# Attention and two experts on one core: two PSUM banks declared independent, all steps in a new order

## The chip, the cores and the metric
The kernel runs on 1 core of a Trainium2 chip. Five engines work side by side, each in the order of its own instruction stream: TensorE (PE, matmuls into PSUM; its weight loads are the rows PEld), VectorE (DVE), ScalarE (ACT), GpSimd (POOL) and SyncE (SP), which issues the DMAs. An instruction starts when the one before it on its engine has been started or is done and the semaphores that it waits for have been raised by other engines. [...]

The metric is the time of one execution on the device in microseconds. A profiled execution of the same kernel gives the trace; its span runs from the first to the last recorded instruction and is a little shorter than the execution's time.

## What is computed
Three stages follow each other. The first is causal attention with a bias from running sums of `s`, for 4 batches, 8 heads, 576 positions and 64 dimensions. The second and third are two experts over the resulting 2304 tokens of 512 values.

```python
# attention, for each batch and head
scores = scale * q @ k.T                     # 576 x 576
cum = cumsum(maximum(s, 0))
scores = where(causal, -1e9, scores + minimum(-(cum[:, None] - cum[None, :]), 0))
attn = exp(scores - max(scores)); attn /= sum(attn) + 1e-9
x = attn @ v                                 # gathered to 2304 x 512
# first expert
h = x @ w_in                                 # 512 -> 2048
x = (h - tanh(h)) @ w_out                    # 2048 -> 512
# second expert
h = x @ w2_in                                # 512 -> 1024
e = exp(h - max(h)); solu = h * e / (sum(e) + 1e-9)
ln = (solu - mean(solu)) / sqrt(var(solu) + 1e-6) * g_ln
out = ln @ w2_out                            # 1024 -> 512
```

All values are float32.

## The kernel before
**Split values.** [...] Each operand is kept as two parts: a rounded one ("hi", written by a CAST, on ScalarE in the rows below) and what is left ("lo", a subtraction, on VectorE in the rows below). A product is then three matmuls: hi times hi, hi times lo, lo times hi. Weights are brought into the same form by some steps on ScalarE and VectorE after their load: a magnitude (line 421), two to four integer steps (lines 403 to 414), a rounding (line 293) and a subtraction (line 317). For the weights w2_out of the second expert a scaling by the gain (line 499) stands in between.

**Attention** takes the heads in pairs. For a pair, TensorE makes the scores (line 719), turns the exponentials by transposes (line 785) and multiplies them with v (line 825); VectorE adds the bias (line 736), ScalarE takes the exponential (line 747) and copies the turned blocks (`pt`), GpSimd divides by the sum (line 751). `bc` is the running sum, spread over the partitions by a DMA from `cum_d`. Ahead of it stand "fillers", matmuls on a tile `junk` whose result nobody reads (line 562).

**First expert** (`expert1`). It works on blocks of 256 tokens, nine of them. Weights for 16 parts f of the hidden width are held in three visits: f 0 to 3 and f 4 to 7 (`VISITS`), whose partial sums go by way of `pd` in DRAM, and f 8 to 15 (the set `wb`). Each f of a block has an h step (line 872, 12 matmuls of 256 columns), a tanh (877), a subtraction (881), a rounding and a rest (293, 317: the tile `gh`), and an x2 step (line 895, 12 matmuls). The weights for `wb` replace buffers of attention, so that their first load (`cd<-in_moe_w_in_dram` at that place) waits for the end of attention. In the last visit line 957 adds the earlier partial sum to the result.

**Second expert** (`products`, `expert2`). For each of the nine blocks of 256 tokens the product with w2_in is made from seven products of half size, p1 to p7, in place of eight, in sums and differences of halves. A product is six matmuls of 512 columns (line 1013). Four of them go to a pair of banks, `big` (`Z["h"]`): p1 and p2 to bank 0, p5 and p3 to bank 1. p6, p7 and p4 go to a bank `b`. Between them the steps are, by their names in the code: k1 copies bank 0 behind p1, u2 = b + k1 (line 1029), k5 copies bank 1 behind p5, k15 adds the two copies (a line 317 with `hc<-hc`), u4 adds u2 into bank 1 (line 1044); then p2 adds into bank 0 and p3 into bank 1. TensorE's order within a block is p1, p6, p5, p2, p3, p7, p4. The two halves of 128 tokens are then two tiles, o = 0 and 1, with the exponential (line 1075), the product with h (1083), mean and variance (1088, 1092), the centring (1095), the reciprocal root (1100 to 1102, then three Newton iterations of three instructions, lines 1107 to 1109, on values of 128x1), eight transposes (1115), the split of what they give (`cd`, `cu`: 293 and 1122, called hi and lo of the first and the second half) and 24 matmuls with w2_out (1129).

**What sets the order.** The kernel first makes a list of 3302 steps, each with one or more ways to be done (on which engine). `ORDER`, a stored text, says in which order the steps are emitted and which way each takes: every word is a number to base 36, three times the step plus the way, and "+n" stands for n fillers. All engines' streams follow from this one order. The costs in the code (`t_pe`, `t_act`, ...) were used when `ORDER` was made; `Plan.order` doesn't use them. Which instruction waits for which follows from the tiles that the instructions read and write, in the order of emission: an instruction that writes a tile waits for the earlier ones of other engines that read or wrote it. The pair of banks is one tile. So u4, which reads and writes bank 1, waits for a p2 that stands ahead of it in the order, which writes bank 0. Whether p2 stands ahead is the order's choice.

## Time and profile before
| what | us |
|---|---|
| median of 3 executions | 791.61 (791.07, 791.61, 792.75) |
| the profiled execution | 792.16 |
| its span in the trace | 790.38 |
| TensorE busy in the span | 771.3 |
| VectorE busy | 541.4 |
| ScalarE busy | 412.6 |
| GpSimd busy | 156.0 |

The profiled execution took 1.8 us more than its span, and lies 0.55 us above the median of the three. An engine's busy time is the time in which at least one of its counted instructions ran; matmuls overlap at their ends, so that TensorE's busy time is not the sum of its matmuls. The granted clock of TensorE was 0.999 of full speed in the mean.

### The profile page before, as it was taken

What the parts mean: (1) busy time and instruction counts of PE and PEld (TensorE: products, weight loads), DVE (VectorE), ACT (ScalarE), POOL (GpSimd) and SP (SyncE); (2) the same over time, 40 slices, a digit from 0 to 9 for tenths busy, and PEclk for the clock granted to TensorE, in tenths of its full rate; (3) what the DMA queues carried; (4) which work ended last, traced back from release to release, by engine and by line L of the source; (5) the groups of instructions that cost most, each with busy time, mean ns of one, the idle gap of its engine ahead of it and who ended that gap; (6) DMA issues with size and microseconds to landing.
All of it is one profiled execution on the core that took longest, in us unless ns stands there. A gap on an engine that the chain in (4) does not pass through costs nothing.

```text
span 790.4 us, 16621 instructions
## 1 busy us (share of the span) xinstructions
PE 771.3 (98%) x6235; PEld 681.0 (86%) x6235; DVE 541.4 (68%) x1521; ACT 412.6 (52%) x1028; POOL 156.0 (20%) x321
## 2 busy tenths in 40 slices
PE   8899999999999999999999999999999999999998
PEld 5565788888898899999999898888899899989876
DVE  6887988854554366985699998765465664564773
ACT  6779988766666445554355664333142333333332
POOL 4334433322331100000000001122041202021112
PEclk9999999999999999999999999999999999999999
DMA  6999979867445379875445431012012101201001
GB/s 189 300 284 252 329 219 290 271 184 215 123 121 165 105 226 292 278 244 181 160 131 183 136 111 48 15 54 92 16 43 65 41 15 66 95 1 41 15 27 41
DMA packets 90033, 111.90 MB, mean 142 GB/s; under 512 B 11792, under 2 KB 74256, under 8 KB 89952
## 3 DMA queue, kind: packets, MB, share of 16 engines
q1 hardware_dynamic: 89952, 110.83, 45.7%
q8 instruction: 49, 0.80, 0.4%
q14 instruction: 32, 0.26, 0.1%
HBM read 87.11 MB, written 23.70 MB: 140 GB/s over the span
## 4 chain that ended last, share of the span: by engine, by line
PE 80%; DVE 10%; ACT 4%; DMA 2%; issue 2%; SPq 1%; POOL 0%; ACTq 0%; DVEq 0%; POOLq 0%
PE t L872 20%; PE t L1129 12%; PE acc L895 11%; PE big L895 10%; PE big L1013 6%; PE t L825 5%; PE t L785 4%; PE b L1013 4%; PE t L719 4%; PE t L1115 2%; ACT U L747 1%; DVE ct L414 1%; DVE U L736 1%; DVE ct L409 1%; ACT pt L293 1%
## 5 line engine op out<-in xcount | busy, mean ns | idle before, releaser
L872 PE MATMUL t<-xb,wih 128*128 128x256 f32 x1152 | 203.4, 279 | 0.1
L872 PEld LDWEIGHTS t<-xb,wih 128*128 128x128 f32 x1152 | 175.6, 188 | 2.2 <-DVE m L736 0.3
L872 PE MATMUL t<-xb,wil 128*128 128x256 f32 x576 | 160.0, 278 | 0.0
L751 POOL TENSOR_SCALAR U<-U,r 128x256 f32<-128x256 f32 (+8 forms) x144 | 85.8, 608 | 174.5 <-DVE r L663 72.9
L872 PEld LDWEIGHTS t<-xb,wil 128*128 128x128 f32 x576 | 108.7, 189 | 0.0
L895 PE MATMUL acc<-gh,woh 128*128 128x256 f32 x576 | 104.7, 283 | 1.2 <-DVE gh L317 1.1
L895 PE MATMUL big<-gh,woh 128*128 128x256 f32 x576 | 101.2, 278 | 0.6 <-DVE xp L957 0.6
L881 DVE TENSOR_TENSOR g<-t,th 128x256 f32<-128x256 f32 x144 | 59.8, 418 | 52.4 <-ACT th L877 51.2
L293 ACT CAST gh<-g 128x256 fp32r<-128x256 f32 x144 | 58.0, 406 | 67.9 <-DVE g L881 30.1
L877 ACT ACTIVATE th<-t 128x256 f32<-128x256 f32 x144 | 55.0, 383 | 71.1 <-PE t L872 66.5
L895 PEld LDWEIGHTS acc<-gh,woh 128*128 128x128 f32 x576 | 87.7, 188 | 3.0 <-DVE gh L317 1.8
L747 ACT ACTIVATE U<-U,m 128x256 f32<-128x256 f32 (+8 forms) x144 | 80.3, 559 | 18.4 <-DVE m L736 17.8
L895 PEld LDWEIGHTS big<-gh,woh 128*128 128x128 f32 x576 | 87.9, 188 | 1.8 <-ACT th L877 0.7
L317 DVE TENSOR_TENSOR gh<-g,gh 128x256 fp32r<-128x256 f32 x130 | 56.4, 436 | 36.2 <-ACT gh L293 35.0
L895 PE MATMUL acc<-gh,wol 128*128 128x256 f32 x288 | 80.4, 279 | 0.2 <-DVE wol L317 0.2
L895 PE MATMUL big<-gh,wol 128*128 128x256 f32 x288 | 79.9, 278 | 0.0
L293 ACT COPY pt<-t 128x512 f32<-128x512 f32 (+4 forms) x160 | 61.2, 427 | 14.1 <-PE t L785 13.1
L736 DVE CUSTOM_DVE_ANT_0 U<-bc,t 128x256 f32<-128x256 f32 (+8 forms) x144 | 60.2, 441 | 5.7 <-PE t L727 3.0
L719 PE MATMUL t<-kn,q 64*64 64x288 f32 (+8 forms) x640 | 59.3, 422 | 1.8 <-ACT pt L293 0.9
L895 PEld LDWEIGHTS acc<-gh,wol 128*128 128x128 f32 x288 | 54.5, 189 | 0.4 <-DVE wol L317 0.4
L895 PEld LDWEIGHTS big<-gh,wol 128*128 128x128 f32 x288 | 54.2, 188 | 0.0
L1107 POOL TENSOR_SCALAR u<-y,va 128x1 f32<-128x1 f32 x45 | 20.9, 465 | 165.1 <-DVE y L1102 137.9
(115 smaller groups left out, 1432.5 us busy)
## 6 DMA issues: line engine op xcount, KB each, us to landing
xb<-xd SPq DMA_DIRECT2D x17, 1024.0 KB, 7.2
cd<-in_moe_w_in_dram SPq DMA_DIRECT2D x24, 512.0 KB, 5.5
cd<-in_moe_w_out_dram SPq DMA_DIRECT2D x24, 512.0 KB, 4.8
bc<-cum_d SPq DMA_DIRECT2D x32, 288.0 KB, 6.4
pd<-xp SPq DMA_DIRECT2D x18, 512.0 KB, 3.0
xp<-pd SPq DMA_DIRECT2D x18, 512.0 KB, 4.1
xd<-xs SPq DMA_DIRECT2D x16, 320.0 KB, 5.1
kn<-in_k_dram SPq DMA_DIRECT2D x16, 288.0 KB, 5.2
```

Source lines behind the costliest of these rows:

```text
L293: nc.scalar.copy(o, i)
L317: return self.any([("dve", t_dve(n, pair=True), lambda: nc.vector.tensor_tensor(*views(), op), "diff-dve"), ("pool", t_pool(n) + split, la ...
L719: nc.tensor.matmul(X[a][c, :z - a], lhsT=V["q"][r, o:o + 64], rhs=V["k"][r, a:z], start=True, stop=True, skip_group_check=True)
L736: nc.vector.tensor_tensor_reduce(out=X["u"][:, a:z], in0=V["bc"][:, n, a:z], in1=X[b][:, a - b:z - b], scale=-0.125, scalar=X["m"] if "m" ...
L747: nc.scalar.activation(out=X["u"][:, :nk], in_=X["u"][:, :nk], func=AF.Exp, scale=-1.0, bias=X["m"], accum_out=Y["s"][:, n:n + 1])
L751: eng.tensor_scalar(X["u"][:, :nk], X["u"][:, :nk], Y["r"][:, n:n + 1], 1.0, ALU.mult, ALU.mult)
L872: nc.tensor.matmul(ps, lhsT=w[l][:, k, f * 128:f * 128 + 128], rhs=xb[:, r, k, :], start=k == 0 and x == 0, stop=k == 3 and x == 2)
L877: nc.scalar.activation(out=X["th", f], in_=X["h", f], func=AF.Tanh)
L881: nc.vector.tensor_tensor(X["g", f], X["h", f], X["th", f], ALU.subtract)
L895: nc.tensor.matmul(X["acc"][:, m, :], lhsT=w[l][:, f, m * 128:m * 128 + 128], rhs=X["gh", f][:, r, :], start=f == c0 and m % 2 == 0 and x ...
L1013: nc.tensor.matmul(o, lhsT=self.x2[j][:, l, x, k], rhs=r[:, b, k, :], start=start and k == 0 and n == 0, stop=k == 1 and n == 2, skip_grou ...
L1129: nc.tensor.matmul(X["po"], lhsT=X["lt", k // 4][:, l, k % 4, :], rhs=r[:, k, :], start=k == 0 and a == 0, stop=k == 7 and a == 2)
```

## The change
Four things change in the code. A function `apart` keeps, for each bank of a block's pair, a list of the instructions that touch it, and declares an instruction independent of those on the other bank that run on another engine (`declare_no_dep`). It is called for the matmuls of p1, p2, p3 and p5, the copies k1 and k5, and u4; for the copies the helper `copy` hands the instruction to a function `then`. The reading of both banks later (line 1070, the exponential and the product with h) is left as it was. Three costs that `Plan.order` doesn't use are other numbers. And `ORDER` is a new text, with the same 3302 steps and 53 fillers for 49. The diff, with `ORDER` cut to a few words:

```diff
 ORDER = """
-0 f x 3 i 10 l u 49 7x p 4i r +22 13 4l 1u 16 2i 86 1a 1c 1x 39 bu 2l 20 2p 6 1f 23 2r 1i 3c 89 1l 2u 4d 26 2x bx 4f
...
+0 f 3 u i l x 49 4i 7x p r +20 13 10 1u 2i 16 86 1a 1c 1x 39 bu 2l 4d 6 2p 1f 20 3c 4l 2r 23 1i 4f 1l 89 3f 2u 26 2x
...
 """
...
-    def copy(self, views, n, psum, deps=(), acq=(), rel=(), ahead=0.0, scale=1.0, engines=("act", "dve", "pool")):
+    def copy(self, views, n, psum, deps=(), acq=(), rel=(), ahead=0.0, scale=1.0, engines=("act", "dve", "pool"),
+             then=lambda inst: None):
...
         def act():
             o, i = views()
-            if scale == 1.0:
-                nc.scalar.copy(o, i)
-            else:
-                nc.scalar.activation(out=o, in_=i, func=AF.Copy, scale=scale)
+            then(nc.scalar.copy(o, i) if scale == 1.0 else nc.scalar.activation(out=o, in_=i, func=AF.Copy, scale=scale))
...
+        def apart(x, inst):
+
+            inst = inst.ins
+            for other in (o for o in Z.setdefault(("h", 1 - x), []) if o.engine != inst.engine):
+                self.tc.declare_no_dep(inst, other, reason="another bank of the pair")
+            Z.setdefault(("h", x), []).append(inst)
...
-                        nc.tensor.matmul(o, lhsT=self.x2[j][:, l, x, k], rhs=r[:, b, k, :], start=start and k == 0 and n == 0,
-                                         stop=k == 1 and n == 2, skip_group_check=True)
+                        i = nc.tensor.matmul(o, lhsT=self.x2[j][:, l, x, k], rhs=r[:, b, k, :], start=start and k == 0 and n == 0,
+                                             stop=k == 1 and n == 2, skip_group_check=True)
+                        if out is not None:
+                            apart(out, i)
...
-            s = add("pe", t_pe(1360.0, 3072), go, deps + list(self.w2_all), acq=acq, rel=rel)
+            s = add("pe", t_pe(1366.0, 3072), go, deps + list(self.w2_all), acq=acq, rel=rel)
...
-        k1 = self.copy(keep1, 512, True, [p1], acq=("hc",))
+        k1 = self.copy(keep1, 512, True, [p1], acq=("hc",), then=lambda i: apart(0, i))
         u2 = add("dve", t_dve(512), sum2, [k1, p6], acq=("u2",))
-        k5 = self.copy(lambda: (c(1), Z["h"][:, 1]), 512, True, [p5, k1])
-        u4 = add("dve", t_dve(512), lambda: nc.vector.tensor_tensor(Z["h"][:, 1, :], Z["h"][:, 1, :], Z["u"], ALU.add), [u2, k5],
-                 rel=("u2",))
+        k5 = self.copy(lambda: (c(1), Z["h"][:, 1]), 512, True, [p5, k1], then=lambda i: apart(1, i))
+        u4 = add("dve", t_dve(512), lambda: apart(1, nc.vector.tensor_tensor(Z["h"][:, 1, :], Z["h"][:, 1, :], Z["u"], ALU.add)),
+                 [u2, k5], rel=("u2",))
...
-        y = self.any([("pool", 1900, lambda: newton(nc.gpsimd), "rstd-pool"), ("dve", 2170, lambda: newton(nc.vector), "rstd-dve")],
+        y = self.any([("pool", 3200, lambda: newton(nc.gpsimd), "rstd-pool"), ("dve", 2170, lambda: newton(nc.vector), "rstd-dve")],
```

In the new text of the kernel the lines of the second expert stand 3 to 5 further down (1013 is 1016, 1029 is 1034, 1044 is 1049, 1095 is 1100, 1107 is 1112, 1115 is 1120, 1122 is 1127), those of the first expert four further up (872 is 868, 877 is 873, 895 is 891), 421 is 417 and 293 is 294. The new order moves steps everywhere; nearly all keep their engine. Of the 18 tiles' Newton iterations, 15 ran on GpSimd and 3 on VectorE; in the new order all 18 are on VectorE.

VectorE, block 8 of the second expert, around u4. Before, from the centring of an earlier tile to the split of that tile:

```order
L1095 TENSOR_SCALAR ct<-ct,mv 128x1024
L1029 TENSOR_TENSOR u_10477<-b,hc 128x512 [waits PE_49]
L317 TENSOR_TENSOR hc<-hc 128x512 [waits Activation_49]
L1044 TENSOR_TENSOR big<-big,u_10477 128x512 [waits DVE_49,PE_49]
L1122 TENSOR_TENSOR cd<-t,cd 128x512 [waits Activation_49]
L1122 TENSOR_TENSOR cu<-t,cu 128x512 [waits Activation_49]
```

The same place in the new order:

```order
L1093 BN_STATS bn<-ct 128x6 [waits DVE_49]
L1034 TENSOR_TENSOR u_10433<-b,hc 128x512 [waits PE_49,Activation_49]
L1093 BN_STATS bn<-ct 128x6
L1127 TENSOR_TENSOR cu<-t,cu 128x512 [waits Activation_49]
L1097 BN_AGGR mv<-bn 128x2 [waits DVE_49]
L1049 TENSOR_TENSOR big<-big,u_10433 128x512 [waits Activation_49]
L1105 TENSOR_SCALAR va<-mv 128x1 [waits DVE_49]
L1106 TENSOR_SCALAR y<-va 128x1 [waits DVE_49]
L1107 TENSOR_SCALAR y<-y 128x1 [waits DVE_49]
L1100 TENSOR_SCALAR ct<-ct,mv 128x1024
L1112 TENSOR_SCALAR u<-y,va 128x1 [waits DVE_49]
L1113 TENSOR_SCALAR u<-u 128x1 [waits DVE_49]
```

The row of u4 (1044, now 1049) listed VectorE and TensorE among what it waits for and now lists ScalarE alone (u4 lists TensorE in 8 of the 9 blocks before, in none after). Behind it the reciprocal root, the centring and the first Newton instructions of a tile now stand on VectorE; before, GpSimd did that tile's iterations. k15 is on GpSimd in three blocks of the new order, this one among them, and on VectorE in the other six.

TensorE, block 8, the matmuls behind p5. Before, p2 begins at the row that waits for ScalarE's copy k1, and p3 at the row that waits for VectorE's u4:

```order
L1013 MATMUL big<-w2ih,x_10333 128x512 [waits Activation_49]
L1013 MATMUL big<-w2ih,x_10333 128x512
L1013 MATMUL big<-w2il,x_10333 128x512
L1013 MATMUL big<-w2ih,x_10333 128x512 x2
L1013 MATMUL big<-w2il,x_10333 128x512
L1013 MATMUL big<-w2ih,x_10333 128x512 [waits DVE_49]
L1013 MATMUL big<-w2ih,x_10333 128x512
L1013 MATMUL big<-w2il,x_10333 128x512
```

In the new order:

```order
L1016 MATMUL big<-w2ih,x_10351 128x512 [waits Activation_49]
L1016 MATMUL big<-w2ih,x_10351 128x512
L1016 MATMUL big<-w2il,x_10351 128x512
L1016 MATMUL big<-w2ih,x_10351 128x512 x2
L1016 MATMUL big<-w2il,x_10351 128x512
L1120 MATMUL t<-idn,ct 128x128 [waits DVE_49,PE_49]
L1120 MATMUL t<-idn,ct 128x128 x3
L1120 MATMUL t<-idn,ct 128x128 [waits PE_49]
L1120 MATMUL t<-idn,ct 128x128 x3
L1016 MATMUL big<-w2ih,x_10351 128x512 x2
L1016 MATMUL big<-w2il,x_10351 128x512
```

Between p2 (the first six matmuls) and p3 (from the ninth row down from the top on, without a wait of its own) now stand the eight transposes of a tile, which stood ahead of p2 before. The transposes wait for VectorE's centring, which stands behind u4 on VectorE.

ScalarE, at the end of attention, from the copy of the first expert's partial sum `xp` on (`th` and `gh` are steps of the first expert, line 421 the magnitude of the first two weights for `wb`). Before:

```order
L293 CAST xs<-t 128x320
L293 COPY xp<-acc 128x1024
L877 ACTIVATE th<-t 128x256
L293 CAST gh<-g 128x256
L877 ACTIVATE th<-t 128x256
L421 ACTIVATE ct<-cd 128x512
L877 ACTIVATE th<-t 128x256
L293 CAST gh<-g 128x256 x2
L877 ACTIVATE th<-t 128x256
L421 ACTIVATE ct<-cd 128x512
```

In the new order:

```order
L294 CAST xs<-t 128x320 x2
L294 COPY xp<-acc 128x1024
L873 ACTIVATE th<-t 128x256
L294 CAST gh<-g 128x256
L873 ACTIVATE th<-t 128x256
L294 CAST gh<-g 128x256
L873 ACTIVATE th<-t 128x256
L417 ACTIVATE ct<-cd 128x512
L873 ACTIVATE th<-t 128x256 x2
L417 ACTIVATE ct<-cd 128x512
```

The first magnitude (421, now 417) stood behind a tanh, a rounding and a tanh, and now stands behind one more of each.

## Rows read from the trace of the kernel before
**Rows 1.** Page, part 1: busy us of each engine, share of the span, instructions
```profile
PE 771.3 (98%) x6235; PEld 681.0 (86%) x6235; DVE 541.4 (68%) x1521; ACT 412.6 (52%) x1028; POOL 156.0 (20%) x321
```

**Rows 2.** Windows: busy us (instructions) by engine, granted clock, DMA share, GB/s
```profile
0.00:130.00 130.00, 121.69 (x1204) 88.20 (x1206) 106.87 (x433) 105.88 (x315) 52.00 (x94) 1.00 0.92 263
...
280.00:320.00 40.00, 38.79 (x336) 38.13 (x334) 28.96 (x63) 19.62 (x45) 1.49 (x2) 1.00 0.84 271
320.00:404.00 84.00, 84.00 (x716) 84.00 (x715) 61.56 (x131) 40.70 (x89) 0.74 (x1) 1.00 0.64 214
404.00:436.00 32.00, 32.00 (x282) 31.85 (x281) 31.60 (x73) 18.83 (x45) 1.64 (x2) 1.00 0.43 132
436.00:500.00 64.00, 61.26 (x438) 56.57 (x437) 58.38 (x129) 34.58 (x69) 4.56 (x11) 1.00 0.30 91
500.00:780.00 280.00, 277.02 (x1732) 246.93 (x1731) 172.25 (x375) 93.81 (x185) 57.49 (x144) 1.00 0.13 42
780.00:791.00 11.00, 6.55 (x29) 5.07 (x27) 1.24 (x2) 1.78 (x3) 0.00 (x0) 0.89 0.13 48
```

**Rows 3.** Waits of TensorE: who waited for whom, us in total, times, longest us
```profile
PE big L1013 <- DVE big L1044: 5.0, 6, 1.4
PE t L785 <- ACT pt L293: 1.6, 2, 0.9
...
PE acc L895 <- DVE gh L317: 1.1, 2, 0.6
...
PE big L895 <- DVE xp L957: 0.6, 1, 0.6
```

**Rows 4.** Timeline, block 8: start us, duration us, instruction, [idle before it <- releaser]
```profile
758.25 0.59 ACT L293 COPY hc<-big 128x512 f32<-128x512 f32 x1 [4.70 <-PE big L1013]
758.87 0.69 DVE L317 TENSOR_TENSOR hc<-hc 128x512 f32<-128x512 f32 x1 [1.66 <-ACT hc L293]
...
760.59 0.70 DVE L1044 TENSOR_TENSOR big<-big,u 128x512 f32<-128x512 f32 x1 [1.02 <-PE big L1013]
...
761.34 0.73 PE L1013 MATMUL big<-w2ih,x 128*128 128x512 f32 x2 [0.79 <-DVE big L1044]
```

**Rows 5.** Timeline, block 0, ScalarE, VectorE and the waiting matmul
```profile
440.11 0.72 ACT L499 ACTIVATE ct<-ct,gain 128x512 f32<-128x512 f32 x1 [1.56 <-DVE ct L414]
...
440.86 0.62 ACT L293 CAST w2oh<-ct 128x512 fp32r<-128x512 f32 x1
...
440.94 0.68 DVE L1029 TENSOR_TENSOR u<-b,hc 128x512 f32<-128x512 f32 x1
...
442.67 0.58 ACT L293 COPY hc<-big 128x512 f32<-128x512 f32 x1
...
444.75 0.73 PE L1013 MATMUL big<-w2ih,x 128*128 128x512 f32 x2 [1.37 <-DVE big L1044]
```

**Rows 6.** The chain that ended last, a DMA on it: start us, us
```profile
277.93 5.70 DMA cd<-in_moe_w_in_dram
```

**Rows 7.** Timeline of ScalarE, the first magnitude for the third visit
```profile
283.87 0.67 ACT L421 ACTIVATE ct<-cd 128x512 f32<-128x512 f32 x1 [3.55 <-DMA cd<-in_moe_w_in_dram]
```

**Rows 8.** VectorE by line, 490 to 780 us: busy us, mean ns, idle before
```profile
L1107 DVE TENSOR_SCALAR u<-y,va 128x1 f32<-128x1 f32 x6 | 1.6, 270 | 0.1
...
L1109 DVE TENSOR_TENSOR y<-y,u 128x1 f32<-128x1 f32 x6 | 1.0, 160 | 0.2
L1108 DVE TENSOR_SCALAR u<-u 128x1 f32<-128x1 f32 x6 | 0.9, 154 | 0.2
```

**Rows 9.** Timeline at the end, 769 to 780 us
```profile
769.27 1.15 ACT L1075 ACTIVATE ct<-hc,m 128x1024 f32<-128x1024 f32 x1 [1.33 <-DVE m L1033]
...
770.33 0.19 ACT L1075 ACTIVATION_READ_ACCUMULATOR ct<-hc,m 128x1 f32 x1
...
775.33 0.74 DVE L1095 TENSOR_SCALAR ct<-ct,mv 128x1024 f32<-128x1024 f32 x1
...
778.70 1.03 PE L1115 MATMUL t<-idn,ct 128*128 128x128 f32 x8
```

More of the change, by code (lines that the diff above doesn't have):

```diff
@@ new lines @@
+37o 1fx 3el 1hi 1ml 37x 1hu 1mf 1ii 37r 3f9 1hl 1g9 1mr 1gc 1mp 37u 1il 1gf 1ho 1ix 1mi 3fo 1g4 1go 1j0 1mu 3ex 3eo
+1mx 1hr 3f0 1j3 3fc 3ff 3f3 1n0 1d0 3f6 3fr 1n9 3fu 3fi 1jc 3fx 1gi 1yi 1d3 3g6 1gl 3g1 1yl 1d9 1d6 3fl 1dc 3g3 3g9
+1ru 3gc 1df 1di 3gl 3bc 1dl 3bf 3gf 1dx 3h3 3gi 1do 380 3bi 1e0 3h6 383 1dr 3bl 1e3 1e6 1nc 3h9 1gr 1e9 1n3 1du 3bo
+3go 1gu 386 39x 3br 389 3hc 1jl 1n6 3bu 1nf 38c 1ni 253 1jo 3hg 38f 1s6 3gr 38l 1nr 1jr 256 1nl 38j 1ju 1nx 1jx 1ec
+1no 1nv 1s9 1yf 3gu 1o0 1sd 1o3 1of 3a0 1o6 3gx 1k0 3a3 1i3 1s3 3a6 1ef 1k3 3a9 1sf 1hx 1i6 3ic 1k6 1i0 3ac 1ki 1ei
@@ new lines @@
+25f 219 25j 106 21l 2ic 109 1sx 21c 263 1t0 21o 10c 1rl 266 21f 25l 1ro 3ix 21r 25o 1rr 10f 25r 21i 1t6 10r 269 26c
+1tc 1ta 3j0 10i 26i 26l 1t3 26g 259 25u 26o 1tf 1ti 26r 3jf 3j6 1tu 1tl 270 1to 110 3ji 1tx 10u 3jl 113 1tr 3ju 1u0
+3jo 3jr 10x 3j9 3ko 3jx 2bl 3k0 3k3 226 3k6 23c 22f 22j 22l 229 2bx 2ox 21u 23f 22c 2ou 10l 23l 23i 22o 25x 23o 3k9
+260 22r 2i6 23r 22u 23u 10o 233 3kr 23x 3kc 240 3kf 21x 220 3ki 249 236 223 3ku 22x 3kl 239 26u 24c 3kx 3nx 26x 2c0
+243 3l0 2c4 24i 3l3 24f 116 24l 246 230 2c6 2c9 2cc 2cf 1u3 2bu 119 1vl 11c 1u6 11f 279 1uc 1u9 2ii 1vo 24o 1ui 2il
@@ L160 @@
+7ar 7hc 72i 7hi 71i 72l 72o 7hl 6tf 7hu 7ho 71l 7hr 71o 7hx 7if 7i0 7i3 7i6 72r 730 7i9 7ic 7bl 733 6ti 7bo 7br 7ii
+6tl 72u 72x 7io 7au 7bu 7il 7ax 7ir 7bx 736 7iu 7b0 7c0 7ix 7j1 739 7c6 7c3 7j3 7ca 73c 73f 7cc 7cl 7cf 7j6 7ci 7co
+7cr 7cu 7jl 7j9 7jo 7jr 7cx 7jc 7ju 7jf 7jx 7d0 7k0 7ji 7d3 7k3 7lf 7k9 7k6 7b3 7kd 7d6 7d9 7kf 7ko 7ki 7li 7b6 7ll
+7kr 7b9 7ku 7lo 7bc 7kl 7lr 7lu 7kx 7lx 7bf 7m0 7bi 7mf 7m4 7m6 7l0 7m9 7mi 7l3 7mc 7ml 7l6 7mo 7l9 7lc 7mr 7mu 7mx
+7n0 7n3
 """
@@ L291, in act @@
             o, i = views()
-            if scale == 1.0:
-                nc.scalar.copy(o, i)
-            else:
-                nc.scalar.activation(out=o, in_=i, func=AF.Copy, scale=scale)
+            then(nc.scalar.copy(o, i) if scale == 1.0 else nc.scalar.activation(out=o, in_=i, func=AF.Copy, scale=scale))
         def dve():
             o, i = views()
-            if scale == 1.0:
-                nc.vector.tensor_copy(o, i)
-            else:
-                nc.vector.tensor_scalar(o, i, scale, None, ALU.mult)
+            then(nc.vector.tensor_copy(o, i) if scale == 1.0 else nc.vector.tensor_scalar(o, i, scale, None, ALU.mult))
         def pool():
@@ L910, in expert1 @@
             if f < c1:
-                s = add("pe", t_pe(1405.0, 12 * TB), lambda f=f: h_part(f), ld + [w["ready"][2 * f]] + list(deps), acq=("ps",),
+                s = add("pe", t_pe(1370.0, 12 * TB), lambda f=f: h_part(f), ld + [w["ready"][2 * f]] + list(deps), acq=("ps",),
                         rel=("xb",) if f == c1 - 1 else ())
@@ L925, in expert1 @@
                 f2 = f - 2
-                s = add("pe", t_pe(1405.0, 12 * TB), lambda f=f2: x2_part(f), [glo[f2], w["ready"][2 * f2 + 1]],
+                s = add("pe", t_pe(1370.0, 12 * TB), lambda f=f2: x2_part(f), [glo[f2], w["ready"][2 * f2 + 1]],
                         acq=("acc",) if f2 == c0 else (), rel=("gh",))
@@ L1157, in expert2 @@
         for k in range(0, 8, 2):
-            s = add("pe", t_pe(1360.0, 3072), lambda k=k: prod(k), [los[k // 4], self.w2_ready[8 + k], self.w2_ready[9 + k]],
+            s = add("pe", t_pe(1366.0, 3072), lambda k=k: prod(k), [los[k // 4], self.w2_ready[8 + k], self.w2_ready[9 + k]],
                     acq=("ps",) if k == 0 else (), rel=(LT[k // 4],) if k % 4 else ())
```

204 lines of the change are left out of this document (95 added, 109 removed).

## The prediction
> **What bounds the kernel now.** I read the page first, then the busy time by stretch, then who waited for whom, and last the instructions around each wait. On the page TensorE is busy 771.3 of 790.4 us, VectorE 68% [rows 1]. So a change to the order can win at most the 19.1 us in which TensorE stands still, and the table by stretch says where they are [rows 2]: 8.3 us in the first 130 us (attention, with VectorE busy 107 us and ScalarE 106), 1.2 us from 280 to 320, none from 320 to 436, 2.7 us from 436 to 500, 3.0 us from 500 to 780, and 3.8 us of the last 10.4. The waits have names [rows 3]: the third product p3 of the second expert waits six times for the VectorE add u4 in the PSUM pair, 5.0 us in all; 1.1 us go to the halves `gh` at 285 us, 0.6 us to the sum of the two halves of the first expert.
>
> The instructions around one of the six show what holds u4 [rows 4]. Its operand is copied from 758.25 to 758.84, the sum beside it ends at 759.56, and VectorE then stands idle 1.02 us until a product into `big` has ended. That product is p2. It writes bank 0; u4 works on bank 1. p3 follows p2 on TensorE at once, so it pays the add in full: 0.79 us idle. The first wait (1.37 us, block 0) has another cause on top: on ScalarE two pairs of scale and round stand between the copies k1 and k5, and k5 starts only at 442.67 [rows 5].
>
> **The change, part by part.** *u4 without the wait for p2.* In the new order u4's row carries no wait for TensorE any more, and in all nine blocks at least 2.7 us of TensorE work (two steps of 1.36 us) stand between the end of p5 and p3. Behind p5 come k5 (0.59), the sum k15 (0.69) and u4 (0.70) [rows 4]: 2.0 us, so the five waits of 0.63 to 0.79 us should go. What hides u4 is then p2 and what stands beside it; without the new order p2 alone covers 1.36 us, and some 0.1 us would be left if k15 is behind u4 and 0.7 us if it is ahead. In block 0 TensorE's order is the same as before. ScalarE has one pair of scale and round (0.72 and 0.62 us) less ahead of k5 [rows 5], but on VectorE one step of a weight conversion (0.68 us) stands between u2 and u4 in place of another; from u2's end at 441.6 I count 0.68 + 0.68 + 0.69 + 0.70 = 2.75, so u4 ends about 444.2 to 444.4 where p3 could start at 443.4. I leave 0.6 us of this wait (bounds 0 and 1.37). In three blocks k15 moves to GpSimd. Its reader is the step behind p7, and p2, p3 and p7 (3 x 1.36 us) stand between: it could take four us there, six times VectorE's 0.69, before anything waited, so I cost it at nothing. Sum: -5.0 + 0.6 = **-4.4 us**.
>
> *The first weights behind attention.* They land at 283.6 [rows 6] and ScalarE, which is in order, sits 3.55 us on the magnitude (line 421) that needs them; two tanh and two roundings are queued behind it, and x2 waits for these halves [rows 7]. In the new order one more rounding and one more tanh stand between the copy of `xp` and the magnitude, and TensorE has seven h steps (9.5 us) after the last attention product instead of five, then three x2 whose halves are ready. Only the fourth x2 comes near: its rounding is still behind the second conversion's. **-1.0 us** of 1.2 (bounds 0 and -1.2).
>
> *The 0.6 us at 465* stay: VectorE is busy 58.4 of 64 us there [rows 2], and its list of work is as long.
>
> *Fifteen Newton iterations from GpSimd to VectorE.* Before, three of eighteen ran on VectorE; now all do. One is three times 270 + 154 + 160 ns [rows 8], 1.75 us, some 2.0 us with the steps between. That is 30 us more VectorE work where it is busy 172 of 280 us [rows 2]: hidden by its idle time, if no iteration stands ahead of something TensorE needs. Two places fail that. In block 1 the iteration of the first tile stands ahead of `lo0` and u4; counted along the rows, both come within 0.1 us of TensorE, and I take 0. At the end, VectorE finished the last tile's centring at 776.07 and the transposes started at 778.70 [rows 9]: 2.63 us of cover. The new order puts one iteration (2.0) and the wait for an exponential (1.15 + 0.2) on this path, 3.3 us, and an iteration ahead of `lo0` in each of the two tiles before. I count 0.6 + 0.2 + 0.2 = **+1.0 us** (bounds 0 and +3.3, if nothing is hidden).
>
> [...]
>
> *Attention's order.* Every step moves, and four more filler matmuls stand among the leading ones (53 for 49). The 8.3 us there are many short waits, the largest group of them two for the copies `pt`, 1.6 us in all and none above 0.9 [rows 3], and the work and its engines are the same. The new order issues the first bias load ahead of the loads of q and v and the first load of the running sums after fewer v loads; against that, four products with v follow their last transpose by only 0.4 to 1.0 us of TensorE work. I see no reason for a sign and take 0, with bounds of -3 and +3: a third of these waits gone, or a third as much again.
>
> *The spacing of equal matmuls.* From 320 to 404 us TensorE fitted 716 matmuls into 84.0 us, 117.3 ns each; from 404 to 436 it fitted 282 of the same kind into 32.0, 113.5 ns, neither with a gap [rows 2]. The slower spacing lasts until some small wait ends it, and costs 2.7 us here. A new order meets other waits. I take it as it is, with bounds of -3 and +4.
>
> Sum: -4.4 - 1.0 + 1.0 = -4.4 us on the profiled execution's 792.16 us (span 790.4 and 1.8 around it), so 787.8; this execution lies 0.55 us above the median of 791.61, so for a median I forecast **787.3 us**.
>
> **The rivals.** *Given back elsewhere.* The waits at u4 go, but attention's new order loses 3 us, or the slow spacing takes the whole stretch to 436 and more. For it: nothing in the rows ties either to the change; against it: most of that stretch is already slow. 790.0 to 793, within 0.2% of before (which is about what a measurement of this kernel can tell from no change).
> *Slower: Newton on the path.* From 436 to 500 VectorE is busy 91%, and there and at the end it now carries about 2.0 us per tile more, ahead of halves that TensorE multiplies next. If more than three iterations in all lie bare (3 x 2.0 = 6 us against 5.4 won), the kernel is slower; with five, 791.6 - 5.4 + 10 = 796. For it: VectorE is in order. Against: from 500 to 780 it idles 108 us, and most of the iterations stand behind the centring and ahead of halves whose rounding has still to come from ScalarE.
> *More than forecast.* The first loads come about 1 us earlier and attention keeps it, or the slow spacing does not set in: 783 to 785.
> *The declaration does nothing*, because the steps stand so that p2 would no longer hold u4 anyway, or another wait holds it. The first would still give the time forecast; for the second nothing in the new rows speaks.
>
> **How the numbers follow.** Forecast (784.9 to 790.0): 0.50. More than forecast: 0.14. Given back: 0.21. Slower: 0.15. Faster by over 0.2% (under 790.0) is 0.50 + 0.14 = 0.64; within 0.2% 0.21; slower 0.15. The range reaches from 783.8, with attention or the spacing at its better bound, to 792.4, where what is won is given back; about 0.08 lies below and 0.12 above. The forecast's own range is 784.9 to 790.0.
>
> **What would show it.** In the waits of the changed kernel, the group of p3 behind u4 should fall from 5.0 us to under 1.0 and hold block 0 alone, and u4's rows should show idle time behind k5 or k15 and none behind a product. The stretch 280 to 320 should idle under 0.4 us. From 500 to 760 TensorE should idle under 1 us and VectorE be busy some 25 us more; the last 30 us should show one to three waits of 0.2 to 0.6 us behind VectorE's centring and halves. I am wrong if TensorE waits in several blocks for `lo0` or the centred tile right behind an iteration, if the first 130 us idle over 11 us, or if p3 still waits for u4 in three blocks or more.

## The result

The new kernel takes 779.34 us (median of 4 runs, 778.90 to 780.52) against 791.43 us (median of 4, 791.07 to 792.75): a ratio of 0.9855, interval 0.9828 to 0.9882. It is faster by 12 us, 8 more than forecast, and lies below the range, and below its outer end of 783.8 us too. The page of the new kernel, span and busy time of the engines (as in [rows 1]):

```profile
span 777.2 us, 16641 instructions
...
PE 764.8 (98%) x6239; PEld 676.8 (87%) x6239; DVE 565.0 (73%) x1647; ACT 409.8 (53%) x1030; POOL 119.5 (15%) x193
```

TensorE idles 12.4 us where it idled 19.1, and is busy 6.5 us less with four fillers more. So half of the gain is not in the idle time at all. To place it I cut both traces at two points of the program, the end of the last attention step on TensorE and the first product of block 0; what lies between them is called the middle stretch below. The windows of the kernel before (columns as in [rows 2]), then of the new one:

```profile
0.00:274.19 274.19, 265.88 (x2666) 212.66 (x2666) 186.35 (x751) 201.00 (x593) 90.08 (x161) 1.00 0.74 217
274.19:436.37 162.18, 160.97 (x1380) 160.16 (x1381) 123.51 (x268) 81.82 (x180) 3.87 (x5) 1.00 0.65 210
436.37:786.55 350.18, 344.46 (x2192) 308.20 (x2190) 231.49 (x504) 129.11 (x255) 62.05 (x155) 1.00 0.16 51
```

```profile
0.00:273.47 273.47, 266.48 (x2694) 214.17 (x2694) 186.84 (x750) 198.64 (x595) 91.86 (x164) 1.00 0.74 219
273.47:429.23 155.76, 154.96 (x1358) 154.23 (x1357) 124.84 (x266) 80.76 (x180) 5.37 (x6) 1.00 0.66 217
429.23:773.08 343.85, 343.33 (x2192) 308.38 (x2190) 253.31 (x632) 129.68 (x255) 22.29 (x23) 1.00 0.16 52
```

The second expert has the same 2192 matmuls in both and takes 6.3 us less. (A step is one unit of the program's order; here 12 matmuls of 256 columns or 6 of 512, 1.36 us of TensorE work either way.) Up to the end of attention the new order does two steps of 12 matmuls more (of the first expert) in 0.7 us less: 0.7 + 2 x 1.36 = 3.4 us. The middle stretch does these two steps less and takes 6.4 us less, 3.7 without them. Sum 13.4; the end behind the last matmul is 0.3 us longer.

The waits of TensorE in the new kernel (columns as in [rows 3]):

```profile
PE t L781 <- POOL U L747: 1.8, 5, 0.5
PE t L715 <- DVE wol L313: 1.3, 1, 1.3
PE acc L558 <- POOL junk L553: 1.1, 1, 1.1
PE acc L891 <- DVE xp L953: 0.7, 1, 0.7
...
PE t L1134 <- DVE cd L1127: 0.4, 1, 0.4
```

The group of p3 behind u4 is gone, and with it `gh` at the first weights and the `xp` of the third visit, whose 0.6 us the prediction expected to stay. The `xp` of the list stands earlier, in the middle stretch. Block 8 around u4, timeline of the new kernel (columns as in [rows 4]):

```profile
740.47 0.59 ACT L294 COPY hc<-big 128x512 f32<-128x512 f32 x1 [0.81 <-PE big L1016]
...
741.14 1.29 POOL L314 TENSOR_TENSOR hc<-hc 128x512 f32<-128x512 f32 x1 [18.04 <-ACT hc L294]
...
741.34 0.67 DVE L1049 TENSOR_TENSOR big<-big,u 128x512 f32<-128x512 f32 x1
...
745.17 0.71 PE L1016 MATMUL big<-w2ih,x 128*128 128x512 f32 x2
```

k5 starts 0.03 us after p5's end, u4 follows it without an idle time of VectorE, and p3 (the last row) comes 3.2 us behind u4's end. k15 on GpSimd takes 1.29 us, within the cover that the prediction gave it.

### The profile page after: what moved, and what is told of

Its sections match the earlier page's. It is cut to its first block, busy times and chain, and to the rows that moved or that the text cites. A ratio compares the mean times of both kernels' runs of the same rounds, so it can differ in the third digit from the quotient of the medians.

```text
span 777.2 us, 16641 instructions
## 1 busy us (share of the span) xinstructions
PE 764.8 (98%) x6239; PEld 676.8 (87%) x6239; DVE 565.0 (73%) x1647; ACT 409.8 (53%) x1030; POOL 119.5 (15%) x193
## 4 chain that ended last, share of the span: by engine, by line
PE 88%; DVE 5%; ACT 2%; DMA 2%; issue 1%; SPq 1%; POOL 0%; DVEq 0%; ACTq 0%; POOLq 0%
PE t L868 23%; PE big L891 13%; PE t L1134 12%; PE acc L891 11%; PE t L821 6%; PE big L1016 6%; PE t L781 5%; PE t L715 5%; PE b L1016 4%; PE t L1120 2%; ACT U L743 1%; DMA bc<-cum_d 1%; DMA cum_d<-pt 1%; ACT pt L294 1%; DVE U L732 1%
## 5 line engine op out<-in xcount | busy, mean ns | idle before, releaser
L747 POOL TENSOR_SCALAR U<-U,r 128x64 f32<-128x64 f32 (+8 forms) x144 | 82.8, 589 | 163.5 <-DVE r L659 50.2
L891 PE MATMUL acc<-gh,woh 128*128 128x256 f32 x576 | 102.6, 280 | 0.8 <-DVE xp L953 0.7
L743 ACT ACTIVATE U<-U,m 128x64 f32<-128x64 f32 (+8 forms) x144 | 80.1, 558 | 21.2 <-DVE m L732 20.7
L313 DVE TENSOR_TENSOR gh<-g,gh 128x256 fp32r<-128x256 f32 x124 | 54.0, 439 | 28.2 <-ACT gh L294 27.1
L732 DVE CUSTOM_DVE_ANT_0 U<-bc,t 128x64 f32<-128x64 f32 (+8 forms) x144 | 60.2, 441 | 8.3 <-PE t L723 6.6
L314 POOL TENSOR_TENSOR gh<-g,gh 128x256 fp32r<-128x256 f32 x20 | 16.5, 827 | 316.9 <-ACT gh L294 249.6
```

The costliest lines, as they stand in the source:

```text
L313: return self.any([("dve", t_dve(n, pair=True), lambda: nc.vector.tensor_tensor(*views(), op), "diff-dve"), ("pool", t_pool(n) + split, la ...
L732: nc.vector.tensor_tensor_reduce(out=X["u"][:, a:z], in0=V["bc"][:, n, a:z], in1=X[b][:, a - b:z - b], scale=-0.125, scalar=X["m"] if "m" ...
L743: nc.scalar.activation(out=X["u"][:, :nk], in_=X["u"][:, :nk], func=AF.Exp, scale=-1.0, bias=X["m"], accum_out=Y["s"][:, n:n + 1])
L747: eng.tensor_scalar(X["u"][:, :nk], X["u"][:, :nk], Y["r"][:, n:n + 1], 1.0, ALU.mult, ALU.mult)
L891: nc.tensor.matmul(X["acc"][:, m, :], lhsT=w[l][:, f, m * 128:m * 128 + 128], rhs=X["gh", f][:, r, :], start=f == c0 and m % 2 == 0 and x ...
```

## The experiments

Seventeen runs; the five with added matmuls stand at the end of this section, the others in the table. For each profile I noted three times between the same points of the program: the end of attention (with the steps of the first expert done by then), the middle stretch, and from p1 of block 0 to the last matmul. Medians of the kernel before vary by up to 2.5 us between groups of runs (790.4 to 792.8), so each ratio is to the kernel before in the run's own group, and the mechanism is read from the profile, which shows one execution.

| run | median us | ratio to before, interval | attention (steps) | middle (steps) | second expert |
|---|---|---|---|---|---|
| before | 791.4 | | 274.1 (70) | 162.3 (115) | 350.2 |
| before again | 791.8 | 1.0002, 0.9984 to 1.0020 | 274.6 (70) | 161.5 (115) | 350.2 |
| new | 779.3 | 0.9855, 0.9828 to 0.9882 | 273.4 (72) | 155.8 (113) | 343.9 |
| new again | 781.6 | 0.9857, 0.9825 to 0.9888 | 274.4 (72) | 155.0 (113) | 343.9 |
| declared only | 787.5 | 0.9943, 0.9923 to 0.9964 | 273.2 (70) | 162.8 (115) | 344.6 |
| order only | 783.9 | 0.9895, 0.9865 to 0.9925 | 275.2 (72) | 159.6 (113) | 345.8 |
| copy not declared | 789.4 | 0.9958, 0.9942 to 0.9973 | 273.9 (70) | 163.1 (115) | 347.1 |
| new from p1 | 784.2 | 0.9914, 0.9895 to 0.9933 | 273.9 (70) | 160.0 (115) | 344.4 |
| new after attention | 782.4 | 0.9891, 0.9866 to 0.9916 | 274.8 (70) | 156.9 (115) | 343.8 |
| new attention, old rest | 788.0 | 0.9935, 0.9905 to 0.9965 | 272.6 (72) | 160.2 (113) | 344.4 |
| new head | 784.8 | 0.9923, 0.9906 to 0.9940 | 273.0 (70) | 162.4 (115) | 344.4 |
| first loads | 787.6 | 0.9945, 0.9926 to 0.9965 | 275.3 (70) | 160.4 (115) | 345.1 |
| Newton on GpSimd, new order | 784.4 | 0.9893, 0.9860 to 0.9926 | 273.8 (72) | 154.6 (113) | 346.8 |
| Newton on VectorE, old order | 795.6 | 1.0074, 1.0048 to 1.0100 | 273.5 (70) | 160.5 (115) | 354.8 |

All carry the declarations but "before", "before again" and "order only"; "copy not declared" lacks one of them.

**Declarations or order.** First each alone; the cut of `ORDER` is against the new kernel.

```diff
 ORDER = """
-0 f x 3 u i l x 49 4i 7x p r +20 13 10 1u 2i 16 86 1a 1c 1x 39 bu 2l 4d 6 2p 1f 20 3c 4l 2r 23 1i 4f 1l 89 3f 2u 26 2x
+0 f x 3 i 10 l u 49 7x p 4i r +22 13 4l 1u 16 2i 86 1a 1c 1x 39 bu 2l 20 2p 6 1f 23 2r 1i 3c 89 1l 2u 4d 26 2x bx 4f
...
```

> The order of before with the declarations alone. Theory A (the gain is three separate parts: about 3.4 us in attention, 3.2 us of faster matmul spacing between attention and the second expert, 5 to 6 us of waits in the second expert, and nearly all of it comes from the order): the waits of p3 behind u4 fall from 5.0 to about 1.4 us, since in blocks 1, 2 and 8 u4 and in blocks 3 and 6 the copy k5 no longer wait for p2, while in block 0 k5 stays behind ScalarE's scaling and rounding; up to the second expert nothing changes, so the slow spacing from 320 to 404 us is there again. Time 787.6 to 788.2 us. Theory B (the declarations are what brings the gain, the rest follows from earlier ends): 780 to 783 us.

787.46 us, as theory A has it. The second expert takes 344.6 us, 5.6 less than before, and the waits at p3 shrink to one line, further than the 1.4 us expected:

```profile
PE big L1015 <- DVE big L1048: 0.3, 1, 0.3
```

```diff
             for other in (o for o in Z.setdefault(("h", 1 - x), []) if o.engine != inst.engine):
-                self.tc.declare_no_dep(inst, other, reason="another bank of the pair")
+                pass
```

> The new order without the declarations. Theory A: in the new order other TensorE work stands between p2 and p3 in every block but the first, which covers a k5 and u4 that start only behind p2; only block 0 pays, about 0.6 us: 779.8 to 780.4 us. Theory B: the waits at p3 come back, 5 us: 784 to 785 us.

Median 783.93 us (780.34 to 786.51), the value of theory B, but not for its reason: the second expert takes 345.8 us, 4.4 less than before, and at p3 only block 0 waits, as theory A has it. One more wait came with the declarations left out, which neither theory named: in block 3 p5, which writes bank 1, waits for ScalarE's copy k1 of bank 0.

```profile
PE big L1016 <- ACT hc L294: 0.7, 1, 0.7
PE big L1016 <- DVE big L1049: 0.6, 1, 0.6
```

Between the profiled executions of this run and of the new kernel lie 7.6 us: 1.9 in the second expert, 1.8 in attention and 3.8 in the middle stretch, which took 159.6 us here and 155.8 in the same order with the declarations, though these touch nothing in it; more on this below. So in the second expert order and declarations each take most of the same waits away: 4.4 and 5.6 us alone, 6.3 together.

**Who waits for p2.** Only the copy k5 is left undeclared in the order of before (the cut is against "declared only").

```diff
-        k5 = self.copy(lambda: (c(1), Z["h"][:, 1]), 512, True, [p5, k1], then=lambda i: apart(1, i))
+        k5 = self.copy(lambda: (c(1), Z["h"][:, 1]), 512, True, [p5, k1])
```

> The order of before with the declarations for the products and u4, not for the copy k5. If u4 alone was held by p2 (as the prediction has it): as the run with all declarations, the waits at p3 in blocks 1, 2, 3, 6 and 8 gone. If in blocks 3 and 6 it is the copy k5 that waits for p2: 0.63 us stays in each of these two, and block 0 keeps 0.3 to 1.4 us, so 1.6 to 2.7 us of waits at p3 and a time 1.3 us above the run with all declarations.

```profile
PE big L1015 <- DVE big L1048: 1.9, 3, 0.6
```

Three waits of 0.6 stay, in blocks 0, 3 and 6: there p2 stood ahead of k5 in the order, and the copy was what waited. The timeline of block 6 in the kernel before shows it (p2 first, an h step behind it, then p3):

```profile
693.66 0.62 PE L1013 MATMUL big<-w2ih,x 128*128 128x512 f32 x2
...
695.23 0.59 ACT L293 COPY hc<-big 128x512 f32<-128x512 f32 x1 [3.50 <-PE big L1013]
...
696.46 0.69 DVE L1044 TENSOR_TENSOR big<-big,u 128x512 f32<-128x512 f32 x1
...
697.21 0.73 PE L1013 MATMUL big<-w2ih,x 128*128 128x512 f32 x2 [0.64 <-DVE big L1044]
```

k5 starts where p2 ends, 1.4 us after p5. It also shows how the view undercounts: from p2's start to p3's are 3.55 us for two steps of 1.36, so the wait cost 0.8, while the row says 0.64, because the ends of matmuls are modelled past the next one's earliest start (in this block the row of a single matmul of p2 lasts 0.39 us, and the next one starts 0.23 us after it began). By starts, each against the shortest time between two such steps, the six waits of the profile before cost 6.1 us, not 5.0: 1.5 in block 0, 1.0 each in blocks 1, 2 and 8, 0.8 each in 3 and 6. With all the declarations 0.4 of this is left, in block 0, which fits the 5.6 us that they give.

**Stage by stage.** The old order up to a seam, the new one behind it, and the other way round; here the words at the first seam, ahead of p1 of block 0.

```diff
-50u 51l 5tc 50x 5br 51o 5si 510 51r 5bu
+50u 51l 5tc 50x 5br 5si 5sl 510 5bu 5c0
...
```

> The order of before up to the first product of block 0, the new order behind it, with the declarations. Theory A: attention and the stretch up to about 436 us take as long as before, with the slow spacing from 320 to 404 us; behind it TensorE idles about 0.5 us instead of 5.7: 784.8 to 786 us. If the gain of the second expert hangs on an earlier start of the others: 787 us or more.

> The order of before up to the last step of attention, the new order behind it, with the declarations. Theory A: attention as before, the stretch from 274 to 436 us with the fast spacing of the new order: 782 to 783.5 us. If the spacing is set by what went before it and not by the order of this stretch, it may be slow again: 785 to 786 us.

> The new order up to the last step of attention, the order of before behind it, with the declarations. Theory A (attention's new order is worth 2 to 4 us of stalls by itself): 2 to 4 us faster than the old order with the declarations, so 783.5 to 785.5 us, with about 17 to 19 us of stalls in attention where the old order has 21. Rival (attention's order is worth nothing, what was seen is chance): within 1 us of the old order with the declarations, 786.5 to 788.5 us. The slow spacing, if it is chance, may be anywhere from 0 to 100 steps behind attention and move the time by up to 5 us.

From p1 on the new order gives 343.8 to 344.4 us wherever it begins, 0.2 to 0.8 less than the old one with the declarations. "New after attention" came out as theory A has it. The three medians (784.2, 782.4, 788.0) don't add up to three separate parts, though: the third, 783.2 to 790.4 us, is by its median no faster than the declarations alone and falls to the rival. Its profiled execution is its fastest, 783.2 us: there attention gains 3.3 us, and TensorE idles 3.5 us in the middle, where the seam lies. What the slower executions lost, no profile shows. And the first run has, up to p1, the order of before, but took 160.0 us in the middle where before took 162.3. Theory A's middle part, a spacing set by the order, is false. The same window of 84 us, in which TensorE does the same kind of work, in the kernel before again, in "new from p1" and in "copy not declared", all with the same order up to there:

```profile
320.00:404.00 84.00, 83.20 (x734) 83.00 (x733) 63.52 (x134) 41.52 (x92) 2.10 (x3) 1.00 0.65 214
```

```profile
320.00:404.00 84.00, 83.25 (x732) 82.86 (x731) 63.61 (x134) 41.38 (x91) 1.65 (x2) 1.00 0.65 214
```

```profile
320.00:404.00 84.00, 84.00 (x715) 84.00 (x715) 61.37 (x129) 41.13 (x89) 0.77 (x2) 1.00 0.63 211
```

734 and 732 matmuls with a wait of 0.8 in between, 715 without any, and 716 in [rows 2]. Counted by step (slow when the median spacing of its matmuls is 0.1165 us or more), the middle has 62, 23, 63, 100, 3, 2, 94 and 6 slow steps in eight profiles of the old order and 2, 0, 97, 0 and 0 in five of the new one. Each slow step costs 0.053 us (1.413 against 1.360), so up to 5 us, and the number changes from one execution of an order to the next. The 97 are those of "order only", whose profiled execution took 786.5 us and its fastest 780.3.

> The new kernel, unchanged, once more. If the slow spacing of the matmuls were set by the order, its profile shows 30 to 40 slow steps of 288 again and the times stay within 778.5 to 781 us. If each execution draws it anew, the number of slow steps differs (anything from 10 to 130) and the times spread over 3 us or more, with a median of 779 to 783 us.

The second half came true: 777.78, 778.74, 779.09, 784.04, 784.06 and 784.66 us, two groups 5.5 us apart; the profiled one, of the first group, has no slow step in the middle. The first four runs of the new kernel were all of that first group. No execution of the second group was profiled; that slow steps make it is inferred from "order only", which has the same order. One window of TensorE in "new again", then in "order only":

```profile
300.00:428.00 128.00, 128.00 (x1127) 127.69 (x1126) 106.72 (x232) 68.52 (x151) 4.35 (x5) 1.00 0.64 210
```

```profile
300.00:428.00 128.00, 128.00 (x1089) 128.00 (x1089) 102.78 (x221) 66.71 (x146) 4.25 (x5) 1.00 0.63 204
```

Both are busy throughout, and 38 matmuls, three steps, lie between them.

> The kernel before, unchanged, once more. If the stalls are fixed by the order and only the spacing is drawn anew in each execution: 21 to 22 us of stalls in attention and 11 to 12 in the second expert, waits of p3 of 4.5 to 5.5 us, and a number of slow steps that may lie anywhere from 20 to 130 (94 in the profile shown).

As expected but for one: 350.2 us in the second expert again and 61 slow steps in all, but p3's waits are 4.3 us, a little under the 4.5 to 5.5, since block 0 waits 0.6 us here and 1.4 there.

**Attention.** The order on the engines in the first 60 us alone, then its first fifteen loads alone.

```diff
-35r tx r9 vc w0 qr u6 12l w3 vi
+35r tx r9 vc w0 u6 qr qu uf qx
...
```

> The new order for the first 60 us (up to the ninth pair's second block of scores), the order of before behind it, with the declarations. If attention's gain is made at its head, where loads and fillers are: 2 to 4 us fewer stalls in attention than the 21.5 of the old order, so 17.5 to 19.5. If it is spread over the whole of attention, or comes from the later part: 20.5 us or more.

```diff
-0 f x 3 i 10 l u 49 7x p 4i r +22 13 4l 1u 16 2i 86 1a 1c 1x 39 bu 2l
+0 f u 3 i l x 49 4i 7x p 10 r +22 13 86 1u 16 2i bu 1a 1c 1x 39 6 2l
...
```

> The order of before with the declarations, and only the first fifteen loads issued in the order that they have in the new kernel (the first bias ahead of the first q and v). If the order of these loads makes attention's gain: 1.5 to 3 us fewer stalls in attention than the 20.5 to 22 of the old order, most of them in the first 30 us. If the gain comes from the order on the engines: within 0.7 us of the old order's stalls.

The stalls of the expectations are counted by step: its time, from its start to the next one's, less the shortest usual time between such two steps. They are some 21 us in attention in the old order, 18.9 with the new head alone and 22.9 with only the first loads in the new order. So the order of the loads isn't what helps, and the new head does stall less. But four more fillers of about 0.24 us stand in it, and the time at which attention ends is the plainer measure. In the seven profiles of the table with attention's old order that is 274.0 us in the mean, and in the five with the new one 271.2 without their two steps more: a gain of 2.8 us. With the new head alone it is 273.0 us, a gain of 1.0. Right behind the seam TensorE idles 2.4 us of ten, 1.3 in the kernel before and 0.5 in the new one; the window in this order:

```profile
60.00:70.00 10.00, 7.63 (x94) 4.83 (x96) 6.31 (x36) 8.18 (x29) 3.45 (x8) 1.00 1.06 299
```

```profile
60.00:70.00 10.00, 8.72 (x89) 5.00 (x81) 7.27 (x38) 8.41 (x30) 5.36 (x9) 1.00 1.03 268
```

```profile
60.00:70.00 10.00, 9.48 (x110) 5.94 (x112) 8.09 (x46) 9.59 (x35) 5.16 (x10) 1.00 0.95 287
```

So the first 60 us are shown to give about a third of the gain. How much of the rest is made behind them and how much this seam costs, and which steps do it, stays open.

**The Newton iterations.** Back on GpSimd in the new order, and all on VectorE in the old one, in each case in the places that they have there.

```diff
-5f9 5fg 5fr 5fi 5ec
+5f9 5ff 5fr 5fi 5ec
...
```

> The new kernel with the fifteen Newton iterations back on GpSimd and every step in the place that it has in the new order. Prediction's view (the iterations on VectorE cost 1.0 us at the end): 0.5 to 1.5 us faster than the new kernel. Theory A (VectorE's idle time hides them): within 0.5 us of the new kernel. Rival (the new order counts on a fast iteration): the outputs, which wait for the scale, come later only at the last tile, 0 to 1 us slower.

```diff
-5fc 6af 6al 5ff 6ao 5dl 6ar
+5fc 6af 6al 5fg 6ao 5dl 6ar
...
```

> The order of before with the declarations, and all eighteen Newton iterations on VectorE, in the places that they have in the order of before. Prediction's view (iterations on VectorE cost where they stand ahead of what TensorE needs): 1 to 3 us more stalls in the second expert than the 5.3 of the run with declarations alone. Theory A (hidden): 5 to 5.6 us of stalls. If GpSimd held up other work in that order too: 0.5 to 2 us fewer.

Neither is free, and both cost more than any of the expectations had it. On GpSimd in the new order the second expert takes 2.9 us longer (346.8): waits come up for a half `gh` that GpSimd makes, and for the operand `x` of the products, in whose sums it has a share:

```profile
PE big L891 <- POOL gh L314: 0.9, 1, 0.9
PE b L1016 <- ACT x L294: 0.8, 1, 0.8
PE b L1016 <- DVE x L313: 0.8, 1, 0.8
```

On VectorE in the old order it takes 10.2 us longer than with GpSimd (354.8 against 344.6), and the kernel is slower than before. One place, timeline of ScalarE, of VectorE and of the matmul that waits:

```profile
657.50 0.59 ACT L293 CAST cd<-t 128x512 fp32r<-128x512 f32 x1 [0.84 <-PE t L1119]
```

```profile
657.77 0.27 DVE L1111 TENSOR_SCALAR u<-y,va 128x1 f32<-128x1 f32 x1
...
659.65 0.16 DVE L1113 TENSOR_TENSOR y<-y,u 128x1 f32<-128x1 f32 x1
659.73 1.28 DVE L1126 TENSOR_TENSOR cd<-t,cd 128x512 fp32r<-128x512 f32 x2
```

```profile
660.46 0.73 PE L1133 MATMUL t<-w2oh,cd 128*128 128x512 f32 x2 [1.18 <-DVE cd L1126]
```

The rounding that this split (`lo0`) needs ended at 658.09 on ScalarE; the iterations stand ahead of it and hold it until 659.73.

**The spacing.** In the ten profiles so far all 272 steps of 512-column matmuls with a step of 256-column ones behind them were followed by the fast spacing. So I added such matmuls, whose result an h step overwrites, in the middle stretch.

```diff
-            ps, xb = self.bank([128, TB]), self.x0 if X["xb"] is None else X["xb"]
-            X["h", f] = ps
+            ps, xb = self.bank([128, 2 * TB]), self.x0 if X["xb"] is None else X["xb"]
+            if (w is self.wb, j, f) in WIDE:
+                nc.tensor.matmul(ps, lhsT=w["ih"][:, 0, f * 128:f * 128 + 128], rhs=xb[:, 0, 0:2, :].rearrange("p k t -> p (k t)"),
+                                 start=True, stop=True)
+            ps = X["h", f] = ps[:, 0:TB]
```

> The new kernel with five added matmuls of 512 columns, one ahead of an h step each (three at about 300 to 350 us, two at the first two blocks of the third visit), into a bank that the h step then overwrites: work that nothing uses, 5 x 0.23 = 1.15 us. In the ten profiles so far a step of 512-column matmuls was followed by the fast spacing 272 times of 272, a step of transposes by the slow one in 48 of 78. Theory C (the spacing is a state that the kind of matmul before sets and that lasts until the next wait or other kind): no slow steps between 300 and 430 us in the profile, and the times in one group, 778.5 to 781 us. Rival (only a wait changes the state): the two groups of the new kernel stay, about 779.5 and 785.5 us.

> The same five added matmuls in the order of before with the declarations, whose other profiles show 62, 63, 3 and 100 slow steps between attention and the second expert. Theory C: 0 to 25 slow steps there (none behind the first added matmul but what a later wait brings), and a median of 785 to 786.5 us against 787.5 without them, with less spread. Rival: 40 or more slow steps and a median of 788 to 789 us.

Medians 780.86 us (779.77 to 781.56, ratio 0.9873, 0.9857 to 0.9889) and 787.97 (0.9960, 0.9942 to 0.9977). Theory C falls in the profile: behind a single wide matmul comes not the fast spacing but the other one. Five windows of 18 us of the first run, one behind each added matmul:

```profile
304.00:322.00 18.00, 18.00 (x161) 18.00 (x160) 14.65 (x30) 9.60 (x21) 0.00 (x0) 1.00 0.77 251
325.00:343.00 18.00, 18.00 (x155) 18.00 (x155) 14.58 (x30) 8.36 (x19) 0.75 (x1) 1.00 0.83 279
349.00:367.00 18.00, 18.00 (x162) 18.00 (x160) 12.90 (x26) 8.48 (x19) 0.00 (x0) 1.00 0.67 233
375.00:393.00 18.00, 18.00 (x155) 18.00 (x154) 13.72 (x31) 9.48 (x23) 0.00 (x0) 1.00 0.72 235
397.00:415.00 18.00, 18.00 (x161) 18.00 (x161) 17.96 (x41) 10.84 (x25) 1.75 (x2) 1.00 0.52 164
```

161, 155, 162, 155, 161: TensorE busy throughout, at the same granted clock, and the spacing turned round five times. The times alone would have passed for theory C: they lie close together, since some half of the stretch is slow whatever it began with. The old order turned at four of its five places. Next, other counts, and matmuls with changing operands:

```diff
-            if (w is self.wb, j, f) in WIDE:
+            for _ in range(WIDE.get((w is self.wb, j, f), 0)):
```

> The new kernel with added matmuls of 512 columns (work that nothing uses) at six places between 300 and 425 us: 2, 1, 2, 1, 3 and 6 of them. The run with single ones showed the spacing change at every one of its five places, slow to fast and fast to slow in turn. If a wide matmul turns the state round each time (theory D): 2 leave it as it was, 1 turns it, 3 turn it, 6 leave it: states behind the places, from a state s before: s, not s, not s, s, not s, not s. If two or more in a row always leave the fast spacing and only a single one turns it (theory E): fast, slow, fast, slow, fast, fast, whatever came before. Theory E agrees with the products' six wide matmuls, which were followed by the fast spacing in every case.

```diff
+            n = WIDE.get((w is self.wb, j, f), 0)
+            for i in range(n):
+                l, r = (("ih", 0), ("ih", 1), ("il", 0))[i % 3]
+                k = i // 3
+                nc.tensor.matmul(ps, lhsT=w[l][:, k, f * 128:f * 128 + 128],
+                                 rhs=xb[:, r, 2 * k:2 * k + 2, :].rearrange("p k t -> p (k t)"), start=i == 0, stop=i == n - 1)
```

> The new kernel with added matmuls of 512 columns as in the run with 2, 1, 2, 1, 3 and 6 of them, but each of a group with other weights and another operand, and added up in the bank, as the products do it: 1, 6, 1, 2, 1 and 3 of them. In the run before, which repeated one matmul, 1 and 3 turned the spacing and 2 and 6 left it. Theory D (only the count matters): turned, kept, turned, kept, turned, turned. Theory F (a group of changing wide matmuls leaves the fast spacing, as behind all 272 steps of the products and of w2_out): fast behind the 6, and behind the 2 and the 3 as well if so few do it; slow behind each single one that follows a fast stretch.

> The new kernel with six added changing wide matmuls at about 300 us alone, 1.36 us of work that nothing uses. Theory F: no slow steps from there to 420 us, times in one group, 779.2 to 780.8 us, against 777.8 to 784.7 in two groups for the new kernel: the median stays or falls by up to 2 us. Theory D: the state is kept, two groups remain, 779.2 to 786 us.

The first two runs are one execution each, 784.41 and 783.99 us. Theory D held at all their twelve places: 1 and 3 turned the spacing, 2 and 6 kept it, changing operands or not. In the third, six stood behind slow steps and fast ones followed, which D doesn't give; its times kept the spread of two groups, as D has it (779.97, 780.58, 782.86 to 785.39; median 783.47, ratio 0.9891, 0.9854 to 0.9927). Why all 272 steps of 512-column matmuls in the ten profiles left the fast spacing is open, and none of these is a better kernel than the new one.

## Why the prediction was wrong

**u4: right in mechanism, too small.** -4.4 us were forecast, and with all else in it the second expert gave -6.3, of which the declarations alone give 5.6. The term was read from the waits' 5.0 us, where the starts say 6.1. Block 0, for which 0.6 us were kept, waits 0.03 by the idle view and 0.2 by starts: k5 started with p5's end, and u4 was done at 436.22, just behind the step before p3. The statement that p2 alone would cover u4 and leave 0.1 to 0.7 us overlooked what stood beside p2 in the old order: eight transposes (blocks 1, 2 and 8) or a step of the first expert (0, 3 and 6). With the declarations alone 0.3 us are left in block 0 by the idle view, and no wait in the others. That u4 alone was held by p2 was half right: in blocks 3 and 6 it was k5, and in block 0 too, where ScalarE came to it in time. u4 on bank 1 beside p2's matmuls on bank 0 took 0.69 us (declared only, block 2) where it took 0.70 alone [rows 4], and three matmuls of p2 beside it 0.68 us, as long as three of p3 behind it. In this trace neither side is slower for the other.

**First weights: right.** -1.0 was forecast for the middle; the wait for `gh` is gone from the list, and idle time in the middle is 0.8 us in one profile of the new kernel (the wait for `xp`) and 0.1 in the other, where it was 1.2. One correction to what stands ahead: not all values are float32. The weight matrices arrive as 64-bit values; the code loads each value as a pair of 32-bit words (`cd`), and the integer steps around the magnitude make float32 of them.

**Newton: the cost was put where it isn't.** +1.0 us was forecast at the end; there stand one wait of 0.4 for `cd` and an end 0.3 us longer (4.1 us behind the last matmul). Both are there as well with the iterations on GpSimd, so neither is theirs. VectorE does carry 22 us more in the second expert, and an iteration takes 1.84 us there (271 + 154 + 187 ns, three times), by its rows in the new kernel (columns as in [rows 8]):

```profile
L1112 DVE TENSOR_SCALAR u<-y,va 128x1 f32<-128x1 f32 x54 | 14.6, 271 | 1.4
...
L1114 DVE TENSOR_TENSOR y<-y,u 128x1 f32<-128x1 f32 x54 | 10.1, 187 | 1.9
L1113 DVE TENSOR_SCALAR u<-u 128x1 f32<-128x1 f32 x54 | 8.3, 154 | 1.9
```

What hides it is the order: in the old places it costs 10.2 us. The rival "Newton on the path" described that kernel, and named the right mechanism. One instruction takes 154 to 271 ns by the rows here, and took 154 to 270 before [rows 8].

**Attention: the step that failed first.** "I see no reason for a sign and take 0." The new order is worth 3.4 us there in the profiled pair (2.8 in the mean of five profiles against seven). The reason given, that waits are short and the work is the same, was none: stalls of some 21 us by step starts stood there, of which the idle view showed 8.3. Which steps of the new order shorten them is not shown.

**Spacing: the step that failed as well.** "I take it as it is." 62 slow steps became 2, 60 x 0.053 = 3.2 us, past the better bound of -3. But this part of the miss is luck as far as these runs can show: the number of slow steps differs between executions of one order, and the second group of the new kernel (784 us) is most likely such executions. Without it, the profiled pair differs by some 10 us.

Forecast and measured, by stage: attention 0 and -3.4, middle -1.0 and -3.7, second expert and end -3.4 and -6.0; -4.4 and -13.1 in all. The range let one of attention and spacing be at its better bound; both were past it, in the same execution. With every part at its own better bound (-0.6 at u4, -0.2, -1.0, -3 and -3) the prediction's sum gives 779.5 us. So the parts allowed for what came, and the range drawn from them did not; its ends, 783.8 and 792.4, don't follow from the bounds either (787.3 - 3 is 784.3).

## What to carry to other kernels

Count a stall from the start of a step to the start of the next, against the shortest such time, before pricing a wait: idle time behind modelled ends showed 5.0 of 6.1 us here and 8.3 of some 21 in attention. A dependency that is only in the bookkeeping can be removed by a declaration or covered by the order, and the two gains don't add (5.6, 4.4, together 6.3). Work that is moved to another in-order engine has no price of its own: the same fifteen iterations cost 2.9 us more on GpSimd than on VectorE in one order, and 10.2 us more on VectorE than on GpSimd in the other.

## What was unexpected of the hardware

TensorE runs the same 12 matmuls of 256 columns in 1.360 or 1.413 us, busy all the time and at the same granted clock of 1.00. In these runs a stretch kept its spacing until a wait or another kind of matmul: in ten profiles 2160 such steps stood behind another such step, and 25 changed the spacing, all but one at a wait. One added matmul of 512 columns turned it round at 14 of 15 places. What in the chip does this, no run here shows.
